# Filter rows ordered by ScalarE before they are turned, late rows turned in pairs, one transform with four residues: a long-convolution and gated-MLP gradient kernel on one core

## The chip, the core and the metric

The kernel runs on one core of a Trainium2 chip. The metric is the device time of one execution in microseconds (us). The five engines are named as in the profile: PE (TensorE; PEld is its weight load), DVE (VectorE), ACT (ScalarE), POOL (GpSimd) and SP (SyncE, which here only issues DMAs). Each engine works through its own instructions in order; semaphores tie the engines together.

## What is computed

The forward pass and all its gradients, for one sequence of S = 2048 rows and D = 1024 columns, F = 3584:

```python
xn = _layernorm(x)                                   # x = A_q
kv = causal_shift(k, shift_k, 4 taps) * v
y  = irfft(rfft(kv, 2S) * rfft(ssm_k, 2S))[:S] + kv * ssm_D      # per column
s  = xn * y
g  = silu(((xn @ w_gate) * (xn @ w_up)) @ w_down)
out = x + s * g
# returned: out and the gradients of x, k, v, shift_k, ssm_k, ssm_D, w_gate, w_up, w_down for grad_out
```

Two parts matter here: the layer norm, with the transposed rows that the product with w_gate and w_up needs, and the Fourier transforms of kv and of the filter ssm_k.

## The kernel before

**Stages.** (1) About 0 to 60 us: the rows of x arrive in six chunks of 1, 1, 2, 4, 4 and 4 blocks of 128 rows. Each chunk is normalised (`layer_norm`) and its rows are transposed into the tiles XNT (U0 to U3), so that they can be the weights of matmuls. (2) Up to about 505 us: slab after slab of w_up and w_gate is multiplied (`gu_unit`, L673: one block is eight matmuls of 128x512 into one of two PSUM buffers `psg`; ACT copies the result out, L675; DVE multiplies its halves into hN; five blocks or more later hN is transposed, L571 or L724). The forward half of the convolution (`conv_forward`) runs between these blocks. (3) About 505 to 700 us: the down projection (L1032) and the gate. (4) From about 700 us: the gradients (L1480, L1497, L1580, L1642).

**The late rows.** The first rows are transposed right behind their normalisation, rows 0 and 1 in two halves (L609), the others whole (L620), and ACT copies them out (L610, L621). All these transposes write one PSUM tile `turns` of four banks, of which `next_bank` hands out one after the other. The chunks of rows 8 to 11 (in U6) and 12 to 15 (in U7) are put on a list and turned by `turn_late`, which `gu_unit` calls behind the first block of a unit: 64 half-transposes for four rows (`turn_halves`, L571: two instructions per 128x128 block, one per 64 partitions) into the whole of `turns`, then four copies by ACT (L631). The layer norm of a chunk is a chain on DVE (statistics L584, L585; L587, L589), one square root on ACT (L592), and DVE again (L595 to L599), which ends in the normalisation of each row (L603).

**The filters.** D is cut into eight slices of 128 columns, ds = 0 to 7. For each one `load_h` brings 128 rows of ssm_k into the first half of U5 as `hrow[p, c, u, r]`: time is 1024c + 8u + r, so that the elements of one residue r lie 8 elements (16 bytes) apart. `h_rows` turns 16 blocks (c, r) with 32 half-transposes. The block is the weight operand of the transpose, so PE itself reads it with that step of 16 bytes. Then ACT copies the result, scaled, into `hx` (L791, two instructions). hx and the shifted product kv of the slice are each transformed: matmuls with a table (`cmm`, L234, 128x256 each), a copy by ACT into SP, then sums on DVE. With eight residues (`fwd8_half`, `fwd8`) this takes 16 matmuls and a longer chain on DVE; with four (`fwd4_half`, `fwd4_sums`, `fwd4_outs`) it takes 32 matmuls and a shorter chain. The list EIGHT names the transforms with eight residues as (slice, 1 for the filter or 0 for kv).

**What sets the order.** A scheduler orders each engine's instructions from the order in which the code issues them and its own costs. The convolution is a generator whose steps yield their planned DVE time; `pump` lets it run ahead in proportion to the blocks that are done (`tick`), with F_TOTAL as the planned whole. DVE's convolution work and some multiplies keep the program's order (`keep_in_program_order`). POOL's queue issues the stores and the loads of k, v and ssm_k.

Of the kernel before, what the change touches and what calls it, by code (L numbers as in the profile page):

```python
# [10 lines left out]
ACT = mybir.ActivationFunctionType  # L11
ALU = mybir.AluOpType
AX = mybir.AxisListType
BF16 = mybir.dt.bfloat16
F32 = mybir.dt.float32
I32 = mybir.dt.int32
PSUM = bass.MemoryType.PSUM


def build_kernel(  # L20
# [498 lines left out]
    fg = pool("fg", 2, side="right")  # L519
    ps_tr = pool("ps_tr", 1, space=PSUM)  # L520
    ps_gu = pool("ps_gu", 2, space=PSUM)
    ps_st = pool("ps_st", 1, space=PSUM)
    turns = ps_st.tile([P, 4, 2, 4, P], BF16, name="tr")
    bank = [0]

    def next_bank():
        bank[0] += 1
        return turns[:, bank[0] % 4]

    busy = turns[:, 0].rearrange("p a b x -> p (a b x)").bitcast(F32).rearrange("p (a x) -> p a x", a=4)  # L530

    def keep_busy(n):
        for i in range(n):
# [33 lines left out]
    def turn_halves(ps, src):  # L567

        for hh in range(2):
            rows = slice(64 * hh, 64 * hh + 64)  # L570
            ins = nc.tensor.transpose(ps(hh), src[rows], ident[rows, rows])  # L571
        return ins

    def halves(x):
        return x.rearrange("p b (h u) -> p h b u", h=2)

    def layer_norm(b0, n, x4):
        def small(name, dt=F32):
            return lns.tile([P, 4], dt, name=name)[:, 0:n]
        mv = lns.tile([P, 4, 2], F32, name="mv")[:, 0:n, :]  # L580
        for i in range(n):
            bst = lns.tile([P, 2, 6], F32, name="bst")
            for hh in range(2):
                V.bn_stats(out=bst[:, hh, :], in_=x4[:, i, hh * 512:(hh + 1) * 512])  # L584
            V.bn_aggr(out=mv[:, i, :], in_=bst[:])  # L585
        var_b = small("var_b", BF16)
        V.tensor_copy(var_b, mv[:, :, 1])  # L587
        vpe = small("vpe", BF16)
        V.tensor_scalar(vpe, var_b, EPS, None, op0=ADD)  # L589
        half_r = small("half_r")  # L590
        with tc.issue_after(act_copy[0].ins) if act_copy[0] is not None else nullcontext():
            root = nc.scalar.activation(half_r, vpe, ACT.Sqrt, scale=0.25)  # L592
        q0 = small("q0")
        rec = small("rec")
        V.reciprocal(rec, half_r)  # L595
        tt(q0, vpe, rec, MUL)
        sq_b = small("sq_b", BF16)
        V.scalar_tensor_tensor(sq_b, q0, 0.25, half_r, op0=MUL, op1=ADD)
        V.reciprocal(RSTD[:, b0:b0 + n], sq_b)  # L599
        for i in range(n):  # L600
            b = b0 + i
            q, qi = divmod(b, 4)
            last = V.tensor_scalar(x4[:, i, :], x4[:, i, :], mv[:, i, 0:1], RSTD[:, b:b + 1], op0=SUB, op1=MUL)  # L603
            if b < 2:
                for hh in range(2):
                    ps = next_bank()[:, 0]
                    for dc in range(4):
                        d0 = (4 * hh + dc) * P
                        tr_ln[0] = nc.tensor.transpose(ps[:, dc, :], x4[:, i, d0:d0 + P], ident[:])  # L609
                    act_copy[0] = nc.scalar.copy(out=XNT[0][:, 4 * hh:4 * hh + 4, b * P:b * P + P], in_=ps)  # L610
                if b == 0:
                    with tc.issue_after(tr_ln[0].ins):
                        keep_busy(10)
                continue
            if b0 >= 8:
                turn_rows.append((x4[:, i, :], q, qi))
                continue
            ps = next_bank().rearrange("p a b x -> p (a b) x")
            for dc in range(DC):
                tr_ln[0] = nc.tensor.transpose(ps[:, dc, :], x4[:, i, dc * P:(dc + 1) * P], ident[:])  # L620
            act_copy[0] = nc.scalar.copy(out=XNT[q][:, :, qi * P:(qi + 1) * P], in_=ps)  # L621
        c, r0 = divmod(b0, 8)
        return last, root, st(xnn[:, c, r0:r0 + n, :], x4[:, 0:n, :])

    def turn_late():
        ps = turns[:].rearrange("p (h j) i b x -> p h j i (b x)", h=2).rearrange("p h j i (a u) -> p h (j i) a u", u=64)
        for i, (x, q, qi) in enumerate(turn_rows):
            for dc in range(DC):
                tr_ln[0] = turn_halves(lambda hh: ps[:, hh, i, dc], x[:, dc * P:(dc + 1) * P])
        for i, (x, q, qi) in enumerate(turn_rows):  # L630
            act_copy[0] = nc.scalar.copy(out=halves(XNT[q][:, :, qi * P:(qi + 1) * P]), in_=ps[:, :, i])  # L631
        turn_rows.clear()

    nop = lambda: None
# [4 lines left out]
    def tr_tile():  # L639
        return ps_tr.tile([P, 2, 8, P], BF16, name="tr")  # L640
# [90 lines left out]
    h_out = []  # L731
    cv_gone = []
    ht_st = [None]
    EIGHT = ((0, 0), (0, 1), (6, 0), (7, 0), (7, 1))
    INV8 = (2, 4, 5, 6, 7)
    SHIFT_W = 8 * 2.3

# [4 lines left out]
    def conv_forward():  # L742
# [33 lines left out]
            st(KSHd[dp], U[6][:].rearrange("p (b d) -> p b d", b=NB))  # L776
            yield 2.3

        def h_rows(ds):
            if ds == 8:  # L780
                return
            hrow = S_["h", ds]
            hx = S_["hx"] = cf.tile([P, NB, P], BF16, name="hx")
            pe_us[0] += 0.67
            ps = tr_tile()[:].rearrange("p h b x -> p h (b x)").rearrange("p h (b u) -> p h b u", u=64)
            with tc.issue_after(tr_ln[0].ins):
                turn_halves(lambda hh: ps[:, hh, 0], hrow[:, 0, :, 0])
            for b in range(1, 16):
                turn_halves(lambda hh: ps[:, hh, b], hrow[:, b // 8, :, b % 8])
            for c in range(2):  # L790
                nc.scalar.activation(halves(hx[:, 8 * c:8 * c + 8, :]), ps[:, :, 8 * c:8 * c + 8], ACT.Copy, scale=WSC)  # L791
            h_out.append(ds)
            if ds + 1 < 8:
                load_h(ds + 1)

        def kvs(ds):
            return S_["kvt", ds // 2][:, :, ds % 2 * P:(ds % 2 + 1) * P]
# [62 lines left out]
        yield from shift(0)  # L860
        PIN[0] = True
        yield 3.9
        h_rows(0)
        yield 0.1
        tl = turn_tables(ps_cv)
        sp = [half(0, S_["hx"], i, Dz[:, 0:P]) for i in range(2)]
        for ds in range(8):
            yield 0.5
            if ds % 2 == 1 and ds < 7:
                with tc.issue_after(S_["kst"].ins):  # L870
                    for c in range(2):
                        load_kv(ds // 2 + 1, c)
            D0 = Dz[:, ds * P:(ds + 1) * P]
            sph = []
            KX = cx.tile([P, 16, 256], BF16, name="KX")
            HX = cs.tile([P, 16, 256], BF16, name="HX", bufs=2)
            own_room = lambda X: X[:].rearrange("p a x -> p (a x)").bitcast(F32).rearrange("p (a x) -> p a x", a=8)[:, 0:4]
            eight = (ds, 1) in EIGHT
            if ds == 0:
                yield from transform(0, 1, sp, HX, own_room(KX), lambda i: sph.append(half(0, kvs(0), i)), nop)  # L880
            else:
                yield from transform(ds, 0, sp, KX, own_room(HX), lambda i: sph.append(half(ds, S_["hx"], i, D0)), nop)
                S_["kst"] = st(KFd[ds], KX[:])
            calls = []

            def behind():
                calls.append(0)
# [3 lines left out]
            yield from transform(ds, int(ds > 0), sph, HX if ds else KX, room, nop1 if eight else lambda c: h_rows(ds + 1) if c == 0 else None,  # L891
                                 behind)
# [80 lines left out]
    st(RSTN[:], RSd.rearrange("(b p) -> p b", p=P))  # L973
    for p_ in (lnp, lns, tg, bsb):
        p_.release()
    ps_st.release()
    ps_cv = pool("ps_cv", 2, space=PSUM)
    pump, drain, step = make_pump(conv, F_TOTAL)
    cnt = [-5]
# [826 lines left out]
```

## Time and profile before

| what | value |
|---|---|
| time, three runs | 1914.03, 1915.66 (median), 1917.43 us |
| the profiled execution | 1915.97 us, of which the span from first to last instruction is 1914.2 us |
| granted PE clock, mean | 0.999 |
| busy: PE, DVE, ACT, POOL | 1895.2, 1550.7, 637.1, 334.8 us |
| PE busy from 100 to 500 us | 397.3 of 400 us |
| PE busy from 20 to 45 us | 19.93 of 25 us |

The profile lists instructions by line of the kernel before, with the tile written and the tiles read (`tr<-ident,U` is a transpose of something in a U tile into the PSUM tile tr). A timeline row gives the start, the time from the first start to the last end of a run of equal instructions, the engine and the line, and in square brackets the idle time of the engine ahead of it with what ended it. A wait row gives the total, the number of times and the longest.

### The profile page before, as it was taken

Reading aid. Unit: us, or ns where it says so; the run is one execution under the profiler, and the core shown is the slowest. Engines: PE = TensorE matmul, PEld = TensorE weight load, DVE = VectorE, ACT = ScalarE, POOL = GpSimd, SP = SyncE. Lnnn points to the kernel's source line nnn. Section 1 sums busy time; section 2 is a strip of 40 time slices with the busy share of each in tenths; the row PEclk is TensorE's granted clock in tenths of the full one; section 3 lists DMA queues with packets and bytes.
Section 4 is the critical chain, followed back from the end, with each engine's and each line's share of the span. In section 5 each row is a group of like instructions: output and inputs, shape, how many; then the busy total and the mean of one; then the engine's idle time right before and its main releaser. Section 6 shows DMA issues by size and latency. Waiting matters only on the chain.

```text
span 1914.2 us, 28265 instructions
## 1 busy us (share of the span) xinstructions
PE 1895.2 (99%) x11367; PEld 1014.8 (53%) x11507; DVE 1550.7 (81%) x1711; ACT 637.1 (33%) x927; POOL 334.8 (17%) x465
## 2 busy tenths in 40 slices
PE   8999999999999999999999999999999999999999
PEld 4555555545444456666666665664444444444444
DVE  7999999999988556887999999999995205678862
ACT  5765555546433233432222222222222102011122
POOL 5121212111113220001031221111212101112120
PEclk9999999999999999999999999999999999999999
DMA  8777866769769997677888698585887999889963
GB/s 285 269 251 232 257 224 207 234 233 296 248 228 311 313 306 230 208 239 229 275 264 264 221 266 267 181 286 177 227 245 173 221 203 180 182 176 195 194 162 124
DMA packets 425107, 444.35 MB, mean 232 GB/s; under 512 B 268400, under 2 KB 342796, under 8 KB 410512
## 3 DMA queue, kind: packets, MB, share of 16 engines
q1 hardware_dynamic: 367504, 239.03, 46.7%
q0 software_dynamic: 41152, 174.15, 29.3%
q10 hardware_dynamic: 16320, 29.36, 4.1%
q8 instruction: 90, 1.47, 0.3%
q14 instruction: 41, 0.34, 0.1%
HBM read 193.87 MB, written 189.84 MB: 200 GB/s over the span
## 4 chain that ended last, share of the span: by engine, by line
PE 96%; DVE 1%; issue 1%; ACT 1%; DMA 1%; SPq 0%; ACTq 0%; DVEq 0%
PE psb L1497 20%; PE psx L1642 20%; PE psg L673 19%; PE psb L1480 10%; PE psb L1580 9%; PE psbm L1032 9%; PE psF L234 3%; PE tr L571 1%; PE psI L455 1%; PE psY L1191 1%; PE psY L445 1%; PE psx L1580 1%; DMA U<-in_A_q_dram 1%; ACT U L631 0%; DVE bst L584 0%
## 5 line engine op out<-in xcount | busy, mean ns | idle before, releaser
L673 PE MATMUL psg<-wslab,U 128*128 128x512 bf16 x1728 | 399.0, 380 | 5.2 <-ACT gut L675 1.2
L1497 PE MATMUL psb<-U,U 128*128 128x512 bf16 x1792 | 397.1, 379 | 0.0
L1642 PE MATMUL psx<-U,dgut 128*128 128x512 bf16 x1505 | 331.0, 379 | 1.6
L1642 PEld LDWEIGHTS <-dgut 128*128 128x128 bf16 x1792 | 175.3, 98 | 211.4
L1497 PEld LDWEIGHTS <-U 128*128 128x128 bf16 x1792 | 175.2, 98 | 198.0
L673 PEld LDWEIGHTS <-U 128*128 128x128 bf16 x1792 | 172.4, 98 | 195.0 <-issue 3.5
L1480 PE MATMUL psb<-wdt,U 128*128 128x256 bf16 x1792 | 205.6, 273 | 0.0
L1480 PEld LDWEIGHTS <-U 128*128 128x128 bf16 x1792 | 175.3, 98 | 29.2
L212 DVE TENSOR_TENSOR W<-W 128x1024 f32<-128x1024 f32 (+1 forms) x189 | 186.5, 1003 | 4.1
L1580 PE MATMUL psb<-U,U 128*128 128x512 bf16 x797 | 176.1, 379 | 0.9
L1502 ACT CAST wb<-psb 128x512 bf16<-128x512 f32 x112 | 65.6, 586 | 315.4 <-PE psb L1497 313.4
L1247 DVE SCALAR_TENSOR_TENSOR dkp<-dkT,kT 128x1024 bf16<-128x1024 bf16 (+2 forms) x64 | 78.3, 1224 | 97.7 <-DMA dkT<-DKSHd 96.0
L1032 PE MATMUL psbm<-U,ht 128*128 128x512 bf16 x658 | 145.0, 379 | 0.7
L1580 PEld LDWEIGHTS <-U 128*128 128x128 bf16 x896 | 87.4, 98 | 104.3
L675 ACT CAST gut<-psg 128x512 bf16<-128x512 f32 x156 | 91.6, 589 | 117.0 <-PE psg L673 108.9
L1674 ACT ACTIVATE dx_t<-dxn 128x1024 bf16<-128x1024 f32 x15 | 15.9, 1057 | 323.1 <-DVE dxn L212 317.7
L1032 PEld LDWEIGHTS <-ht 128*128 128x128 bf16 x672 | 65.6, 98 | 78.2
L212 DVE TENSOR_TENSOR U<-U,dht 128x2048 bf16<-128x2048 bf16 x56 | 68.3, 1221 | 46.8 <-ACT dht L1482 46.7
L1482 ACT CAST dht<-psb 128x512 bf16<-128x512 f32 x112 | 65.6, 587 | 116.3 <-PE psb L1480 116.3
L66 POOL DMA_DIRECT2D Hd<-hN x54 | 37.3, 690 | 261.2 <-DVE hN L212 259.0
L1621 ACT CAST wbs<-psb 128x512 bf16<-128x512 f32 x51 | 29.9, 586 | 145.4 <-PE psb L1580 134.4
L212 DVE TENSOR_TENSOR W<-SP 128x1024 f32<-128x1024 f32 x64 | 74.2, 1218 | 1.6 <-ACT SP L295 1.1
(259 smaller groups left out, 2342.2 us busy)
## 6 DMA issues: line engine op xcount, KB each, us to landing
U<-GUd SPq DMA_DIRECT2D x28, 1024.0 KB, 8.9
DGd<-U SPq DMA_DIRECT2D x28, 1024.0 KB, 6.2
GUd<-gut ACTq DMA_DIRECT2D x39, 512.0 KB, 5.8
out_dram<-wb SPq DMA_DIRECT2D x112, 128.0 KB, 4.9
U<-Hd SPq DMA_DIRECT2D x14, 1024.0 KB, 6.7
Hd<-hN POOLq DMA_DIRECT2D x54, 256.0 KB, 5.0
HTd<-hT SPq DMA_DIRECT2D x24, 512.0 KB, 4.1
ht<-HTd SPq DMA_DIRECT2D x18, 512.0 KB, 7.6
```

What stands on the lines that cost most here:

```text
L212: pinned(V.tensor_tensor(o, a, b, op))
L234: mm = nc.tensor.matmul(ps[:, k].rearrange("p (c d) -> p c d", c=2), T[:, r, k, :], xr[:, r], start=(n == 0), stop=(n == len(rs) - 1 and ( ...
L673: gu_mm[0] = nc.tensor.matmul(ps[:], XNT[q][:, dc, qi * P:(qi + 1) * P], w[:, dc].rearrange("p a f -> p (a f)"), start=(dc == 0), stop=(dc ...
L675: nc.scalar.copy(out=gut[:, :, i], in_=ps[:].rearrange("p (a f) -> p a f", a=2))
L1032: mm = nc.tensor.matmul(ps[:, dh * 512:(dh + 1) * 512], ht(fc)[:, i * P:(i + 1) * P], WD[fc // 4][:, fc % 4, dh * 512:(dh + 1) * 512], sta ...
L1247: ins = V.scalar_tensor_tensor(prod[:].rearrange("p r d -> p (r d)")[:, lo:H], dkT[:, 0, lo:H], 1.0, kT[:, 0, 13 + m + lo:13 + m + H], op0 ...
L1480: nc.tensor.matmul(ps[:, x * SLW:(x + 1) * SLW], DBMT[2 * hf + g][:, dc, (b % 4) * P:(b % 4 + 1) * P], wdt[:, dc, :], start=(dc == 0), sto ...
L1482: nc.scalar.copy(out=dht[:, 2 * e:2 * e + 2].rearrange("p b f -> p (b f)"), in_=ps[:])
L1497: nc.tensor.matmul(ps[:], XN[b // 4][:, b % 4, dc * P:(dc + 1) * P], dgus[b // 8][:, :, b % 8], start=(b == 0), stop=(b == NB - 1))
L1502: nc.scalar.copy(out=wb[:, dc % 2].rearrange("p a f -> p (a f)"), in_=ps[:])
L1580: nc.tensor.matmul(ps, h[:, f, b, :], DBM[b // 4][:, b % 4, dh * 512:(dh + 1) * 512], start=(b == 0), stop=(b == NB - 1))
L1642: nc.tensor.matmul(ps[:, dh * 512:(dh + 1) * 512], t[n][:, f, i * P:(i + 1) * P], WGU[n][:, f, dh * 512:(dh + 1) * 512], start=(n == 0 and ...
```

## The change

- The first transposes get PSUM buffers of their own: the tile `turns` becomes a pool of four single-bank buffers.
- `turn_late` releases that pool and takes one with two buffers of two banks, each for two rows: two rows are turned and copied, then the next two.
- For slices 1 to 7 the filter rows are first ordered by residue: ACT reads hrow with the step of 16 bytes and writes hx (`h_order`, scaled, two instructions). Then the 32 half-transposes read hx, whose elements are contiguous, and ACT copies the result back into hx (`h_turn`). The two halves of the work are called at two steps of the convolution. Slice 0 keeps the order of before, but with 16 whole transposes in place of 32 half ones.
- (6, 0) leaves EIGHT: kv of slice 6 is transformed with four residues.

```diff
-    ps_st = pool("ps_st", 1, space=PSUM)
-    turns = ps_st.tile([P, 4, 2, 4, P], BF16, name="tr")
+    ps_st = [pool("ps_st", 4, space=PSUM)]
...
-                    ps = next_bank()[:, 0]
+                    ps = ps_st[0].tile([P, 4, P], BF16, name="tr")
...
-            ps = next_bank().rearrange("p a b x -> p (a b) x")
+            ps = ps_st[0].tile([P, DC, P], BF16, name="tr")
...
     def turn_late():
-        ps = turns[:].rearrange(...)
-        for i, (x, q, qi) in enumerate(turn_rows):
-            for dc in range(DC):
-                tr_ln[0] = turn_halves(lambda hh: ps[:, hh, i, dc], x[:, dc * P:(dc + 1) * P])
-        for i, (x, q, qi) in enumerate(turn_rows):
-            act_copy[0] = nc.scalar.copy(out=halves(XNT[q][:, :, qi * P:(qi + 1) * P]), in_=ps[:, :, i])
+        if turn_rows and len(ps_st) == 1:
+            ps_st[0].release()
+            ps_st.append(pool("ps_s2", 2, space=PSUM))
+        for i in range(0, len(turn_rows), 2):
+            ps = ps_st[1].tile([P, 2, 2, DC, 64], BF16, name="tr2")
+            for j, (x, q, qi) in enumerate(turn_rows[i:i + 2]):
+                for dc in range(DC):
+                    tr_ln[0] = turn_halves(lambda hh: ps[:, hh, j, dc], x[:, dc * P:(dc + 1) * P])
+            for j, (x, q, qi) in enumerate(turn_rows[i:i + 2]):
+                act_copy[0] = nc.scalar.copy(out=halves(XNT[q][:, :, qi * P:(qi + 1) * P]), in_=ps[:, :, j])
...
-    EIGHT = ((0, 0), (0, 1), (6, 0), (7, 0), (7, 1))
+    EIGHT = ((0, 0), (0, 1), (7, 0), (7, 1))
...
-        def h_rows(ds):
+        def h_order(ds):
...
+            if ds > 0:
+                for c in range(2):
+                    nc.scalar.activation(hx[:, 8 * c:8 * c + 8, :], hrow[:, c].rearrange("p u r -> p r u"), ACT.Copy, scale=WSC)
+                if ds + 1 < 8:
+                    load_h(ds + 1)
+
+        def h_turn(ds):
...
+            if ds == 0:
+                ps = tr_tile()
+                for b in range(NB):
+                    ...
+                        nc.tensor.transpose(ps[:, b // 8, b % 8, :], hrow[:, b // 8, :, b % 8], ident[:])
+                    if b % 8 == 7:
+                        nc.scalar.activation(hx[:, b - 7:b + 1, :], ps[:, b // 8], ACT.Copy, scale=WSC)
+                load_h(1)
+            else:
+                ps = tr_tile()[:]...
+                for b in range(NB):
+                    turn_halves(lambda hh: ps[:, hh, b], hx[:, b, :])
+                for c in range(2):
+                    nc.scalar.copy(out=halves(hx[:, 8 * c:8 * c + 8, :]), in_=ps[:, :, 8 * c:8 * c + 8])
...
-            yield from transform(..., nop1 if eight else lambda c: h_rows(ds + 1) if c == 0 else None, behind)
+            yield from transform(..., nop1 if eight else lambda c: (h_order, h_turn)[c](ds + 1), behind)
...
-            if eight:
-                h_rows(ds + 1)
+            if eight:
+                h_order(ds + 1)
...
-            yield from product(KX, HX, KX, cs, False, 0)
+            steps = product(KX, HX, KX, cs, False, 0)
+            yield next(steps)
+            if eight:
+                h_turn(ds + 1)
+            yield from steps
```

More of the change, by code (lines that the diff above doesn't have):

```diff
@@ L521, in build_kernel @@
     ps_gu = pool("ps_gu", 2, space=PSUM)
-    ps_st = pool("ps_st", 1, space=PSUM)
-    turns = ps_st.tile([P, 4, 2, 4, P], BF16, name="tr")
[L524 to L530, printed above, removed]
+    ps_st = [pool("ps_st", 4, space=PSUM)]
+    busy = ps_st[0].tile([P, 4, P], F32, name="tr")
     def keep_busy(n):
@@ L609, in layer_norm @@
                         tr_ln[0] = nc.tensor.transpose(ps[:, dc, :], x4[:, i, d0:d0 + P], ident[:])
-                    act_copy[0] = nc.scalar.copy(out=XNT[0][:, 4 * hh:4 * hh + 4, b * P:b * P + P], in_=ps)
+                    act_copy[0] = nc.scalar.copy(out=XNT[0][:, 4 * hh:4 * hh + 4, b * P:b * P + P], in_=ps[:])
                 if b == 0:
@@ L617, in layer_norm @@
                 continue
-            ps = next_bank().rearrange("p a b x -> p (a b) x")
+            ps = ps_st[0].tile([P, DC, P], BF16, name="tr")
             for dc in range(DC):
                 tr_ln[0] = nc.tensor.transpose(ps[:, dc, :], x4[:, i, dc * P:(dc + 1) * P], ident[:])
-            act_copy[0] = nc.scalar.copy(out=XNT[q][:, :, qi * P:(qi + 1) * P], in_=ps)
+            act_copy[0] = nc.scalar.copy(out=XNT[q][:, :, qi * P:(qi + 1) * P], in_=ps[:])
         c, r0 = divmod(b0, 8)
@@ L625, in turn_late @@
     def turn_late():
-        ps = turns[:].rearrange("p (h j) i b x -> p h j i (b x)", h=2).rearrange("p h j i (a u) -> p h (j i) a u", u=64)
-        for i, (x, q, qi) in enumerate(turn_rows):
-            for dc in range(DC):
-                tr_ln[0] = turn_halves(lambda hh: ps[:, hh, i, dc], x[:, dc * P:(dc + 1) * P])
-        for i, (x, q, qi) in enumerate(turn_rows):
-            act_copy[0] = nc.scalar.copy(out=halves(XNT[q][:, :, qi * P:(qi + 1) * P]), in_=ps[:, :, i])
+        if turn_rows and len(ps_st) == 1:
[8 more added lines that the diff above has]
+                act_copy[0] = nc.scalar.copy(out=halves(XNT[q][:, :, qi * P:(qi + 1) * P]), in_=ps[:, :, j])
         turn_rows.clear()
@@ L783, in h_rows @@
             hx = S_["hx"] = cf.tile([P, NB, P], BF16, name="hx")
-            pe_us[0] += 0.67
[L785 to L791, printed above, removed]
+            if ds > 0:
[4 more added lines that the diff above has]
+        def h_turn(ds):
+            if ds == 8:
+                return
+            hx = S_["hx"]
+            pe_us[0] += 0.67
+            if ds == 0:
+                hrow = S_["h", 0]
+                ps = tr_tile()
+                for b in range(NB):
+                    with tc.issue_after(tr_ln[0].ins) if b == 0 else nullcontext():
+                        nc.tensor.transpose(ps[:, b // 8, b % 8, :], hrow[:, b // 8, :, b % 8], ident[:])
[3 more added lines that the diff above has]
+            else:
+                ps = tr_tile()[:].rearrange("p h b x -> p h (b x)").rearrange("p h (b u) -> p h b u", u=64)
+                for b in range(NB):
+                    turn_halves(lambda hh: ps[:, hh, b], hx[:, b, :])
+                for c in range(2):
+                    nc.scalar.copy(out=halves(hx[:, 8 * c:8 * c + 8, :]), in_=ps[:, :, 8 * c:8 * c + 8])
             h_out.append(ds)
-            if ds + 1 < 8:
-                load_h(ds + 1)
         def kvs(ds):
@@ L862, in conv_forward @@
         yield 3.9
-        h_rows(0)
+        h_order(0)
+        h_turn(0)
         yield 0.1
@@ L890, in conv_forward @@
             room = cf.tile([P, 4, 256], F32, name="room", tag="hx")[:] if eight else None
-            yield from transform(ds, int(ds > 0), sph, HX if ds else KX, room, nop1 if eight else lambda c: h_rows(ds + 1) if c == 0 else None,
+            yield from transform(ds, int(ds > 0), sph, HX if ds else KX, room, nop1 if eight else lambda c: (h_order, h_turn)[c](ds + 1),
                                  behind)
@@ L975, in build_kernel @@
         p_.release()
-    ps_st.release()
+    ps_st[1].release()
     ps_cv = pool("ps_cv", 2, space=PSUM)
```

## The prediction

> **What bounds the kernel.** I read the busy times first, then the chain that ended last, then PE's waits.
>
> ```profile
> PE 1895.2 (99%) x11367; PEld 1014.8 (53%) x11507; DVE 1550.7 (81%) x1711; ACT 637.1 (33%) x927; POOL 334.8 (17%) x465
> ...
> PE 96%; DVE 1%; issue 1%; ACT 1%; DMA 1%; SPq 0%; ACTq 0%; DVEq 0%
> ...
> PE tr L620 <- DVE U L603: 3.2, 1, 3.2
> PE psg L673 <- ACT gut L675: 1.2, 1, 1.2
> PE tr L609 <- ACT U L610: 0.9, 2, 0.7
> ```
>
> PE is the bound from the first microseconds to the end. So the change can win in two ways only: less time of PE's own instructions, or less of PE's idle time, which lies almost all ahead of 60 us. Other engines matter where they make PE wait. The timeline of PE gives the prices:
>
> ```profile
> 147.56 1.17 PE L571 MATMUL tr<-ident,U 64*128 64x64 bf16 x32
> 148.66 1.90 PE L673 MATMUL psg<-wslab,U 128*128 128x512 bf16 x7
> ...
> 155.69 0.64 PE L571 MATMUL tr<-ident,hN 64*128 64x64 bf16 x32
> 156.27 1.04 PE L673 MATMUL psg<-wslab,U 128*128 128x512 bf16 x3
> ...
> 471.14 1.04 PE L234 MATMUL psF<-kv,TF 128*128 128x256 bf16 x8
> 472.01 5.34 PE L673 MATMUL psg<-wslab,U 128*128 128x512 bf16 x24
> ```
>
> From the start of a group to the start of the next: 32 half-transposes of filter rows (tile U, step of 16 bytes) hold PE for 1.10 us, 32 of hN (contiguous) for 0.58, unrounded 1.098 and 0.574. Eight transform matmuls cost 0.87. The weight loads say why; in one stretch of 100 us:
>
> ```profile
> L571 PEld LDWEIGHTS <-hN x160: 92/95/96, 311.7 to 388.4; 64*128 64x128 bf16 x160
> L571 PEld LDWEIGHTS <-U x64: 137/165/170, 322.9 to 374.7; 64*128 64x128 bf16 x64
> ```
>
> The start is shown by rows of DVE, PE and ACT:
>
> ```profile
> 18.63 1.88 DVE L584 BATCH_NORM_STATS2 bst<-U 128x6 f32<-128x512 bf16 x3 [2.00 <-DMA U<-in_A_q_dram]
> 20.43 1.04 DVE L212 TENSOR_TENSOR hN_s<-gut_s 128x256 bf16<-128x256 bf16 x1
> 21.39 0.20 DVE L585 BATCH_NORM_AGGREGATE mv<-bst 128x2 f32<-128x12 f32 x1
> ...
> 27.00 0.62 PE L620 MATMUL tr<-ident,U 128*128 128x128 bf16 x8 [3.19 <-DVE U L603]
> ...
> 36.03 0.22 ACT L592 ACTIVATE half_r<-vpe 128x4 f32<-128x4 bf16 x1
> 39.53 3.76 ACT L631 COPY U<-tr 128x1024 bf16<-128x1024 bf16 x4 [1.77 <-PE tr L571]
> ...
> 43.83 3.61 PE L673 MATMUL psg<-wslab,U 128*128 128x512 bf16 x16 [1.21 <-ACT gut L675]
> ```
>
> A multiply of 0.28 us (its neighbours at 16.15 and 16.35) takes 1.03 at 20.43, in the middle of the layer norm of rows 4 to 7 and beside POOL's four copies of 17.06 to 21.27. PE waits 3.19 us for that chain. The next chunk's square root stands ready at 34.98 and runs at 36.03, behind two copies of ACT. Then four copies of ACT in a row keep PE waiting for 1.21 us.
>
> **1. Filter rows.** Seven slices go from 1.098 to 0.574 us on PE: 7 x 0.524 = **-3.7**. Slice 0 gets 16 whole strided transposes for 32 half ones: between a contiguous whole one (0.056, L620) and a load that nothing overlaps (0.163, the median strided load), 0.9 to 2.6 us against 1.1. I take the pair of strided halves, 1.098/16 = 0.069 each: **0**, bounds -0.2 and +1.5.
>
> Added on ACT: 14 activations that read with the step of 16 bytes. No row has ACT reading so. From below: a contiguous activation of 1024 elements, 1.04 us (L964); from above: twice that. ACT is 57% busy from 100 to 500 us, so the 15 to 29 us fit. Behind each one waits the copy of a slab block (0.59), and PE waits for that copy when it is late by more than ACT's usual idle time of 1.14 us ahead of it, since PE fills the other PSUM buffer in 1.73. The built order of the changed kernel spreads them: the two of a slice have a slab copy between them, and in most slices 16 transform matmuls (0.87 to 1.75 us) follow on PE before the buffer is wanted. Laid out by hand for slices 2 to 4 with 1.04, and for 2 and 4 with 2.08, PE keeps a margin of 0.1 us or more. So **0**; without that cover, 14 x (2.08 - 1.14) = +13. Below 0 it can't go, nothing is taken from ACT's path. The transposes of hx wait for ACT, but stand a step of the convolution (several blocks of 1.73) behind. On POOL each `load_h` now waits for ACT instead of PE; its data are wanted a slice, some 50 us, later, and the waits of that kind (POOL U L66 <- PE tr L571) total 13.3 us today without holding PE.
>
> **2. Slice 6.** 16 more matmuls of 128x256, two groups of 0.87: **+1.75** on PE. DVE loses about 6 us: the chain with eight residues at 74.62 to 90.96, less a multiply of 0.61, takes 15.7; the one with four has the same first 4.6 and four sums of 1.22. DVE isn't on the path; it gets slack, of which part 3 takes some. PE's tightest DVE input is a kv tile, ready 1.47 us ahead of its matmuls at 302.93; by counting both orders PE comes to them 1.35 later in its own work and DVE has one multiply (0.6) more, so the wait stays away. 0, or up to +1 if DVE lags.
>
> **3. The start**, laid out on the new order with old durations. First half-rows: PE no longer waits for ACT (0.67 and 0.24), but the first matmuls of the second slab still wait for its DMA at 14.59: nothing gained yet. Rows 4 to 7: the slow multiply now stands ahead of the statistics, in DVE's idle 2.00 us, so the chain ends 0.96 earlier, and rows are ready at 26.0, 26.45, 26.9 and 27.35. PE has 41 matmuls of 0.216 and 18 transposes of 0.055 from 14.59 on, arrives at 24.4, and finishes the four rows at 27.9. Then 29 matmuls and six small transposes: 34.5. DVE's next chain is 0.96 earlier, and 0.20 for a wait at 34.02 that falls away: its square root stands ready at 33.8. ACT has done its copies at 32.3, so it runs at once, 2.2 earlier than 36.03. Row 8 is ready at 35.5, row 11 at 36.8; PE waits 1.0 and has turned them at 37.2. ACT copies the first two rows from 36.3 to 38.15, the others to 40.0, the slab block to 40.5: PE goes on at 40.5 where it was 43.83. **-3.3**. The same pairing at rows 12 to 15 takes the wait of 0.34 at 57.89: **-0.3**. Bounds: 0, if the slab, the rows' DMA or another multiply sets the pace again; and -7, all idle time from 23.8 to 58 us (5.3) and half of the 3.4 us at half clock. I stay with the schedule, which lies between. Everything later keeps step: DVE starts its shift some 3.4 earlier, since what it waits for (ACT's copy, PE's turn, k's load behind a store of rows 8 to 11) moves too.
>
> A row on the clock: the granted clock of 28.0 to 31.4 us, right behind PE's wait of 3.19, is 0.51. [...] If it halves again, PE loses up to 1.7 of work, of which the wait of 1.0 at 34.5 hides 1.0: +0.7.
>
> **Sum.** -3.7 + 0 + 1.75 - 3.3 - 0.3 = -5.5 us. The profiled execution took 1915.97 (span 1914.2, 1.77 around it), 0.3 over the median of 1915.66. Forecast: **1910.4**.
>
> **Rivals.**
> A, the start gives nothing back: another wait replaces the one at 27.00. For: DMA is nearly full there, and the rows of a chunk are now turned together, so PE waits for the last of four. Against: the rows land at 18.6 and the chain is DVE's own. -3.7 + 1.75: 1914.0.
> B, the turn isn't faster, because writing into PSUM and not the weight load sets 1.10 us: -3.6 + 1.75: 1914.1. Against: the two L571 groups differ in the weights' step alone.
> C, slower: ACT's strided read costs as PE's does. Longest strided to contiguous load, 173/95: 1.89 us each. If the slab copy stands right behind each, PE waits 0.75 at each of 14: +10.5, so 1920.9. It eats the whole gain from 1.53 us per activation on (5.5/14 over 1.14) and is slower by over 0.2% from 1.79, if the cover counted in part 1 fails at nearly all of them.
> [...]
>
> **Chances.** Forecast 0.63, A 0.2, B 0.05, C 0.12. Range 1907.9 to 1915: below, a start that gains 5.9 and slice 0 at -0.2 (1907.9); above, A with slice 0 at +1.5 (1915.5, cut a little); C is left out. About 0.2% (3.8 us, to 1911.8) is what a measurement can tell from no change. Forecast falls under faster, A and B under same, C under slower.
>
> **What would show it.** Half-transposes of hx at 0.57 us a group; PE's wait near 27 us halved and the waits of 0.67 and 1.21 gone or shorter, the block of 43.83 near 40.5; 32 matmuls for kv of slice 6; the ordering activations near 1.04 us; no new PE wait on ACT. A wait `PE psg <- ACT` counted some 14 times would make it wrong (C), as would a wait on L603 that stays at 3 us (A).

## The result: 1921.5 us, slower than before by 0.3%

The changed kernel took **1921.52 us** (median of 8 runs, 1919.65 to 1923.69) beside 1915.28 for the kernel before in the same job (8 runs): ratio 1.0031, interval 1.0021 to 1.0040. Forecast were 1910.4, and a range up to 1915. The profiled execution took 1923.45, span 1921.7 against 1914.2 before.

The first part of the page and PE's waits (total, times, longest) of the changed kernel, in its profiled execution:

```profile
PE 1901.1 (99%) x11507; PEld 1011.7 (53%) x11507; DVE 1544.9 (80%) x1699; ACT 662.2 (34%) x941; POOL 334.6 (17%) x465
```

```profile
PE psg L671 <- ACT U L673: 6.3, 4, 2.3
PE psx L1661 <- DVE dxn L212: 2.6, 1, 2.6
PE psg L671 <- ACT gut L673: 2.2, 4, 0.9
...
PE tr L614 <- DVE U L597: 0.9, 1, 0.9
```

PE's busy time can't be set against the 1895.2 of before: that profile lists 11367 of PE's instructions beside 11507 weight loads, this one 11507 of each. Before, PE's only wait above 1.5 us was the one of 3.2 in the start. That one is now 0.9 (1.6 forecast). In its place stand waits of the slab product (`psg`) for ACT. The ordering activations and the copy behind the turn, from the rows of the tile hx:

```profile
L784 ACT ACTIVATE hx<-U x14: 2045/2130/2150, 103.6 to 448.9; 128x1024 bf16<-128x1024 bf16 x14
L807 ACT COPY hx<-tr x14: 1012/1017/1042, 112.8 to 455.0; 128x1024 bf16<-128x1024 bf16 x14
```

2.13 us (median) with the step of 16 bytes, 1.02 for as many elements without it. The forecast had taken 1.04 and looked at 2.08 for two slices only. Slice 1 is the worst place; first ACT's timeline, then PE's:

```profile
103.56 2.08 ACT L784 ACTIVATE hx<-U 128x1024 bf16<-128x1024 bf16 x1 [2.66 <-DVE KX L283]
105.54 0.58 ACT L673 CAST U<-psg 128x512 bf16<-128x512 f32 x1
106.00 1.88 ACT L193 COPY TI<-psT 128x2048 bf16<-128x2048 bf16 x1
107.76 2.04 ACT L784 ACTIVATE hx<-U 128x1024 bf16<-128x1024 bf16 x1
```

```profile
102.73 1.89 PE L671 MATMUL psg<-wslab,U 128*128 128x512 bf16 x8
106.17 1.89 PE L671 MATMUL psg<-wslab,U 128*128 128x512 bf16 x8 [1.55 <-ACT U L673]
110.33 1.89 PE L671 MATMUL psg<-wslab,U 128*128 128x512 bf16 x8 [2.28 <-ACT U L673]
```

ACT stands still for 2.66 us in front of the first activation, because hx of slice 1 gets the buffer that DVE still uses as scratch (`room`, tag "hx", L905) for the eight-residue transform of slice 0. The slab copies (L673, from psg) queued behind are late, PE has filled both PSUM buffers and waits 1.55 and 2.28 us.

To see where the time goes, I compared the start of the same slab block in both traces (the 16th, the 32nd and so on; each block has 8 weight loads): after minus before is -3.9 us at the 16th and -4.0 at the 32nd (the start has won), -0.3 at the 48th (slice 1 has taken 3.7 back), and +3.3 at the first matmul of the down projection. From there it stays +3.3 to 1610 us, where a wait of 2.57 and a stretch at a granted clock of 0.57 make it +7.5. (That is the profiled execution, one of the slowest of the eight; the medians lie 6.2 apart.)

### The profile page after: what moved, and what is told of

Its sections match the earlier page's. It is cut to its first block, busy times and chain, and to the rows that moved or that the text cites. A ratio compares the mean times of both kernels' runs of the same rounds, so it can differ in the third digit from the quotient of the medians.

```text
span 1921.7 us, 28410 instructions
## 1 busy us (share of the span) xinstructions
PE 1901.1 (99%) x11507; PEld 1011.7 (53%) x11507; DVE 1544.9 (80%) x1699; ACT 662.2 (34%) x941; POOL 334.6 (17%) x465
## 5 line engine op out<-in xcount | busy, mean ns | idle before, releaser
L673 ACT CAST gut<-psg 128x512 bf16<-128x512 f32 x156 | 91.6, 592 | 117.7 <-PE psg L671 108.4
```

What stands on the lines that cost most here:

```text
L673: nc.scalar.copy(out=gut[:, :, i], in_=ps[:].rearrange("p (a f) -> p a f", a=2))
```

## Experiments

Ratios stand against the kernel before, run in the same job. Waits, leads and lines are of one profiled execution of each kernel. The lead is how much earlier than before the same slab block starts.

**Rows as before: start and four residues only**

```diff
 # the change without h_order / h_turn
-            h_order(ds + 1) ... h_turn(ds + 1)
+            h_rows(ds + 1)
```

> The changed kernel with the filter rows turned as before (PE reads them with the step of 16 bytes, ACT orders nothing); the new start and the four residues of slice 6 stay. Theory READ: the 14 ordering activations of the changed kernel take 2.13 us each, twice what a contiguous read takes, and PE then waits for slab copies queued behind them, 8.1 us in all between 100 and 480 us. Then this kernel gets the start's -3.9 and the +1.75 of slice 6: 1915.3 - 3.9 + 1.75 = 1913.1, and PE has no wait on ACT over 0.5 us after 60 us. Rival PACE: the smaller planned total and the four residues move the convolution's steps against the slab blocks, and that makes PE wait, whatever ACT reads: about 1921, with the waits of the changed kernel.

Measured 1915.23, ratio 1.0002 (0.9993 to 1.0011). Without the ordering 6 us of loss are gone; the new pace alone doesn't make the loss. But it is 2 above READ, and PE waits 0.68 us for ACT at 472 us, where READ had nothing over 0.5.

**Rows only**

```diff
 # the kernel before, with h_order / h_turn and nothing else of the change
-            h_rows(ds + 1)
+            h_order(ds + 1) ... h_turn(ds + 1)
```

> The kernel before with the ordering and turning of the filter rows alone changed. READ: -3.7 on PE for the turn, +8.1 or a little more of waits on ACT: 1919.7 to 1921, with ordering activations of 2.1 us and PE waiting behind them by 1 to 2 us in several slices. PACE: no such waits, 1915.3 - 3.7 = 1911.6.

Measured 1920.95, ratio 1.0032 (1.0019 to 1.0044). The ordered rows by themselves cost as much as the whole change, with eight residues in slice 6 too. READ's time holds. Its 8.1 us of waits are 6.6 here: 1.36 and 1.51 in slice 1, the second for hx itself at the turn, and the rest near 265, 380 and 451 us.

**Start only**

```diff
 # the kernel before, with the PSUM pool and turn_late of the change only
-    turns = ps_st.tile([P, 4, 2, 4, P], BF16, name="tr")
+    ps_st = [pool("ps_st", 4, space=PSUM)]
```

> The kernel before with the transposes of the first and late rows alone changed (own PSUM buffers, turned in pairs). READ and PACE alike: the start's -3.9 stays to the end, 1911.4, since PE is the bound throughout. Rival GIVEN BACK: PE that is ahead meets the same later time of a DMA (as it waits for DVE near 1612 us in the changed kernel), and the end moves by less than 1 us: 1914.5 to 1915.3.

Measured 1912.00, ratio 0.9986 (0.9978 to 0.9995). The lead is 3.1 us at the 32nd block and 3.1 at the end: nothing is given back.

**Ordering activation with a contiguous read**

```diff
-hx[:, 8 * c:8 * c + 8, :], hrow[:, c].rearrange("p u r -> p r u")
+hx[:, 8 * c:8 * c + 8, :].rearrange("p b u -> p (b u)"), hrow[:, c].rearrange("p u r -> p (u r)")
```

> The changed kernel, but the 14 ordering activations read the filter rows contiguously, so the rows are not ordered by residue and the filter's values are mixed up; every instruction and tile is otherwise the same. READ: the activations take 1.04 us, PE's waits behind them go, but for slice 1, where ACT stands 2.7 us waiting for DVE: 1915.3 - 3.9 - 3.7 + 1.75 = 1909.5, up to 1911.8 with that wait. PACE: the step of the read does not matter, about 1921.

Measured 1916.66, ratio 1.0009 (1.0000 to 1.0018). The activation takes 1.07 us (median) in place of 2.13, and the kernel is 4.9 us faster than the changed one, where READ had some 10 to 12: READ is half right. PE's waits that are left:

```profile
PE psg L671 <- ACT gut L673: 3.9, 4, 1.7
PE psg L671 <- ACT U L673: 1.9, 2, 1.3
```

Of the first row 0.94 and 0.20 lie ahead of 75 us; the others stand in slice 1 (0.57, 1.31) and slice 7 (1.69, 1.03). So a pair of activations makes PE wait even at half the length, where ACT is busy or held up anyway. From here on the theory is LOAD: not the length alone, but where the added work stands in ACT's queue.

**Four residues only**

```diff
-    EIGHT = ((0, 0), (0, 1), (6, 0), (7, 0), (7, 1))
+    EIGHT = ((0, 0), (0, 1), (7, 0), (7, 1))
```

> The kernel before with (6,0) taken from the list EIGHT and nothing else. LOAD (the loss of the whole change is PE waiting for slab copies of ACT that stand behind the added ordering activations; the four residues cost their 16 matmuls alone): 1915.2 + 1.8 = 1917.0. Rival FOUR (the kernel with the start and the four residues was timed 3.2 us over the one with the start alone, so the four residues also bring a wait in slice 7): 1918.4 or more, with a PE wait on ACT near 470 us.

Measured 1918.38, ratio 1.0017 (1.0008 to 1.0026): 3.5 over before, FOUR's side of the two. PE's own work grows by 1.8, as forecast; a wait of 1.03 near 474 us on ACT is new. In ACT's timeline:

```profile
469.58 1.07 ACT L675 CAST gut<-psg 128x512 bf16<-128x512 f32 x2 [3.77 <-DMA GUd<-gut]
```

ACT's slab copy can't write, because a store of the buffer `gut` has not landed; then two slab copies, two into hT and two into the tile SP (not the engine) stand in a row, 4.6 us, until the next slab copy at 474.16. Before, the same wait of ACT was 2.47 us and cost PE nothing.

**Own scratch for slice 0**

```diff
-room = cf.tile([P, 4, 256], F32, name="room", tag="hx")[:] if eight else None
+room = (U[7][:, 0:2048].bitcast(F32)... if ds == 0 else cf.tile([P, 4, 256], F32, name="room", tag="hx")[:]) if eight else None
```

> The changed kernel, with DVE's scratch tile 'room' of slice 0 in U7 instead of the buffer that hx of slice 1 needs, so that the first ordering activation of slice 1 no longer waits 2.66 us for DVE. LOAD: the two PE waits of slice 1 (1.55 and 2.28) shrink by about 2.6 together, all other waits on ACT stay: 1921.5 - 2.6 = 1918.9. Rival STRIDE ALONE (the two waits come from the 2.05 us of each activation, the wait for DVE lay beside other work): 1921.5, the two waits as before. Where the late dkT transpose of the changed kernel's profile (PE wait of 2.57 and a half clock behind it, 4.1 together) is chance, it is absent in some profiles, and the time is up to 4 lower in either case.

Measured 1915.93, ratio 1.0005 (0.9997 to 1.0014), 5.6 below the changed kernel. The activations still take 2.12 us, but both waits of slice 1 are gone (3.8 us, more than LOAD's 2.6), and so, in this profile, is the late wait at 1610 us. The two waits don't make up all of the 5.6; the rest may be that late wait, which the median of the changed kernel can hold in part, but no run shows it apart. What is left on ACT, but for one of 0.20 at 74 us, stands in slices 4 (0.76, 0.74), 6 (1.70) and 7 (0.22, 0.84).

**Ordering on POOL**

```diff
-nc.scalar.activation(hx[...], hrow[:, c].rearrange("p u r -> p r u"), ACT.Copy, scale=WSC)
+nc.gpsimd.tensor_copy(hx[...], hrow[:, c].rearrange("p u r -> p r u"))
```

> The start of the change and its filter rows, kv of slice 6 with eight residues as before, but POOL orders the filter rows (the scale moves to ACT's copy behind the turn). LOAD: ACT has no added work, so PE keeps the whole gain of the turn: 1912.0 (start alone) - 7 x 0.524 = 1908.3, with no PE wait on ACT above 1 us after 60 us. Rival PORT (POOL's copies, about 2 us each by half the 4.1 us of its 128x2048 copies, slow DVE beside them as they slowed a multiply from 0.28 to 1.03 us, and PE waits for DVE): 1910 or more, with PE waits on DVE in slices 1 to 7. Rival KEPT (the turn of contiguous rows gives PE nothing on the whole): 1912.

Measured 1952.93, ratio 1.0197 (1.0183 to 1.0211). Wrong by 45 us for LOAD, and not as PORT had it either: POOL is the one that is held up. Rows of the copy, then of PE's waits:

```profile
L784 POOL COPY hx<-U x14: 1974/2400/20214, 104.2 to 480.9; 128x1024 bf16<-128x1024 bf16 x14
```

```profile
PE tr L565 <- POOL hx L784: 27.6, 6, 13.2
```

One copy took 20.2 us, from 388.7 us on, and PE waited 13.2 us for it; DVE was busy for 18.4 of them. The next copy, with DVE idle, took 1.97. But the twelve others, beside a busy DVE too, took 2.1 to 10.0 us, and what makes the difference was not tried.

**Four pieces behind slab copies**

```diff
+            slab = nc.scalar.copy(out=gut[:, :, i], in_=...)
+            if pieces:
+                with tc.issue_after(slab.ins):
+                    pieces.pop(0)()          # 128x512, half of one activation
...
+            h_order(ds + 1)                  # ahead of the second transform; room of slice 0 in U7
```

> The start and the filter rows with eight residues for slice 6; ACT orders as in the change, but in four pieces of 512 elements a slice (about 1.07 us each by half of 2.13), each placed right behind one slab copy, the first a step of the convolution earlier ('room' of slice 0 in U7). ACT has the same work as in the change. LOAD: a piece fits into ACT's usual idle time of 1.14 us behind a slab copy, so the waits of the pairs go: 1908.3 to 1910. Rival TOTAL (ACT's added 29 us, not where it stands, makes PE wait): 1914 or more, with PE waits on ACT of some 5 us in all after 100 us.

Measured 1917.35, ratio 1.0017 (1.0008 to 1.0026). A miss for LOAD as forecast, but the waits have changed:

```profile
PE tr L565 <- ACT hx L788: 3.9, 6, 1.1
...
PE tr L565 <- ACT hT L709: 1.8, 2, 0.9
```

From 60 to 500 us the slab blocks wait for ACT only twice, by 0.20 and 0.32. PE now waits at the turn, for the last piece.

**Every slice another step**

```diff
+R = (8, 8, 2, 4, 16, 32, 8, 1)
-hrow[:, c].rearrange("p u r -> p r u")
+hrow[:, c].rearrange("p u r -> p (u r)").rearrange("p (u r) -> p r u", r=R[ds])
```

> The changed kernel with another step of reading in each slice's two ordering activations (slices 1 to 7: 16, 4, 8, 32, 64, 16 and 2 bytes), 1024 elements and the same place in the program each time; the filter values are mixed up by it. [...] Rival STEP (the cost grows with the step): between 1.07 and 2.13 at 4 and 8 bytes, above 2.13 at 32 and 64. [...]

Measured 1920.19, a single execution. ACT's timeline gives the second activation of slices 1, 3 and 4, with steps of 16, 8 and 32 bytes:

```profile
108.01 2.04 ACT L786 ACTIVATE hx<-U 128x1024 bf16<-128x1024 bf16 x1
...
209.92 1.20 ACT L786 ACTIVATE hx<-U 128x1024 bf16<-128x1024 bf16 x1
...
262.42 2.13 ACT L786 ACTIVATE hx<-U 128x1024 bf16<-128x1024 bf16 x1
```

Slices 2 (4 bytes) and 7 (2 bytes) took 1.06 and 1.07, slice 5 (64 bytes) 2.00 and 2.05, slice 6 (16 bytes) 2.11 and 2.07. PE's waits of slices 1, 4 and 6 stayed as they were in the changed kernel. STEP falls: the cost doesn't grow with the step. 4 bytes cost no more than 2, 8 bytes 1.20, and 16, 32 and 64 bytes all about double (2.00 to 2.13).

**Pieces, and the turn a step later**

```diff
 # over the kernel with four pieces
-lambda c: h_turn(ds + 1) if c else None        # in the transform
+nop1
...
             yield next(steps)                   # first step of the product
-            if eight:
-                h_turn(ds + 1)
+            h_turn(ds + 1)
```

> The kernel with four pieces a slice, and the turn of the ordered rows one step of the convolution later in every slice (behind the first step of the product), so that PE comes to it when the last piece is done. LOAD: the waits of the hx turn for ACT (3.9 in all) go, the slab copies stay on time: 1917.4 - 3.9 - some of the 1.8 of waits for hT's copy = 1912 to 1913.5. If the turn of contiguous rows gives PE its whole 3.7 and no wait takes its place: 1908.3. Rival MOVED (what PE doesn't wait for at the turn it waits for at the next copy of ACT, since the same 33 us of ACT lie in the same stretch): 1916 or more.

Measured **1910.31**, ratio 0.9979 (0.9970 to 0.9988): faster than before and than the changed kernel. From 60 to 500 us PE has no wait above 0.2. The pieces took 1.16 us each, so ACT does even more work than in the change. MOVED falls: the same amount of ACT's work in the same slices costs PE no wait up to 500 us when each piece stands behind a slab copy, slice 0 has its own scratch and PE comes late enough.

**Own scratch and contiguous read**

```diff
 # over the kernel with own scratch: the contiguous read from above
-hrow[:, c].rearrange("p u r -> p r u")
+hrow[:, c].rearrange("p u r -> p (u r)")
```

> The changed kernel with 'room' of slice 0 in U7 and, besides, the ordering activations reading their rows contiguously (the order is left out, the filter values are mixed up). LOAD: without the doubled length the waits of slices 4 and 6 (0.76, 0.74 and 1.70) go as well, those of slice 7 stay (1.1 to 2.7, one of about 0.7 to 1.0 is of the four residues): 1915.9 - 3.2 = 1912.7, up to 1914 if slice 7 waits as with the contiguous read before. Rival STRIDE NOTHING (with the wait for DVE gone, the length of the activation no longer matters): 1915.9.

Measured 1914.27, ratio 0.9995 (0.9986 to 1.0004). The waits of slices 4 and 6 (3.2 us) are gone, as LOAD has it; slice 7 takes 2.91 and 1.03, near LOAD's upper case. ACT's timeline there:

```profile
460.10 0.52 ACTq L72 DMA_DIRECT2D GUd<-gut  x1
466.73 1.07 ACT L673 CAST gut<-psg 128x512 bf16<-128x512 f32 x2 [6.66 <-DMA GUd<-gut]
```

The store that ACT waits for was issued at 453.19 and landed 12.9 us after its issue had ended (in the kernel before, the store issued at 448.60 took 7.5). It went out right behind SP's loads of HTd into U at 451.45; that these delay it was not tried. In the four kernels with the ordering in pairs and four residues at the same pace, the waits of slice 7 grow with the lead at the 192nd block: 1.0 us in all at a lead of 1.3, 1.1 at 5.2, 2.7 at 6.7 and 3.9 here at 9.3. The kernel with pieces and the late turn (eight residues, lead 6.1) has none, so the lead alone doesn't make them.

**The whole change with the good place**

```diff
 # the kernel with pieces and the late turn, and
-    EIGHT = ((0, 0), (0, 1), (6, 0), (7, 0), (7, 1))
+    EIGHT = ((0, 0), (0, 1), (7, 0), (7, 1))
```

> The whole change (start, ordered filter rows, four residues for kv of slice 6), with the one difference from it that ACT's ordering stands where the last kernel has it: four pieces behind slab copies, the turn a step later, 'room' of slice 0 in U7. PLACE (the change lost its gain by where ACT's ordering stands, not by the strided reads as such, nor by the four residues beyond their matmuls): 1910.3 + 1.8 = 1912.1, up to 1913.1 with the wait of 0.7 to 1.0 in slice 7 that two kernels with four residues showed. Rival FOUR (the four residues bring DVE's chains and ACT's copies of slice 7 together so that more is lost): 1914 or more, with PE waits on ACT of 2 us or more near 465 to 475 us.

Measured 1916.66, ratio 1.0009 (1.0000 to 1.0018): 4.9 below the changed kernel, but 4.6 above PLACE. PE waits 0.91 and 0.91 for copies of hT, 2.00 at 351 us and 1.65 at 468 us. The one at 351, in ACT's timeline:

```profile
348.72 1.93 ACT L709 COPY hT<-tr 128x1024 bf16<-128x1024 bf16 x2 [2.96 <-DMA HTd<-hT]
```

Again ACT stands behind a store that has not landed (hT has one buffer), and the slab copies behind it are late.

**The same, at the pace of eight residues**

```diff
-    F_TOTAL += len(EIGHT) * (FWD8_W - 9.6 + 0.95 * 1.75) - 2.0
+    F_TOTAL += (len(EIGHT) + 1) * (FWD8_W - 9.6 + 0.95 * 1.75) - 2.0
```

> The kernel with four residues and well placed pieces, with the planned whole of the convolution (F_TOTAL) as with eight residues for slice 6, so that its steps stand against the blocks of the slab product as in the kernel of pieces and late turn (1910.3). PACING (the four residues cost 4.5 us beyond their matmuls because a smaller F_TOTAL moves every step of all slices to other blocks, and there ACT's copies meet stores that haven't landed): 1910.3 + 1.8 = 1912.1 to 1913.2, the PE waits at 153, 331 and 351 us gone, one in slice 7 possible. Rival WORK (the second 16 matmuls and SP copies themselves bring the waits): 1915 or more.

Measured 1916.98, ratio 1.0012 (1.0003 to 1.0021). Half of PACING is right: the waits at 153, 331 and 351 us are gone, and at the 176th block the lead is 6.3 us (6.1 in the best kernel). Then, in slices 6 and 7 (from the 176th to the 208th block), all of it and more goes:

```profile
PE psg L672 <- DMA wslab<-in_B_w_gate_dram: 3.5, 2, 2.5
PE psF L234 <- ACT SP L256: 1.6, 1, 1.6
```

The wait of 2.5 for the slab's own load (at 455 us) is followed by a stretch of 3.4 us at a granted clock of 0.56, which costs some 1.5 more (an estimate: 3.4 x 0.44). Together with the 16 matmuls (1.8) that is about 7.4 of the 7.9 us that are lost there. By time alone WORK wins; by the trace, pace and work each have their part.

**The changed kernel at the pace of before**

```diff
 # the changed kernel with the F_TOTAL of the diff above
```

> The changed kernel with the same planned whole as before (F_TOTAL counted with five transforms of eight residues). PACING: the waits of slices 4, 6 and 7 come at other places or sizes; those of slice 1 (3.8) stay, since hx waits for 'room' there; the four residues no longer shift all steps: 1921.5 less up to 4. Rival PLACE ALONE (the ordering pairs make PE wait wherever they stand): 1920 to 1922, waits on ACT of 7 us or more in all.

Measured 1922.78, ratio 1.0037 (1.0024 to 1.0051). Pace doesn't save the changed kernel. The waits for ACT above 0.3 us, after 60 us, sum to 5.8 (1.38, 1.50, 0.75, 0.74, 1.38), under PLACE ALONE's 7; one of 2.95 for a slab's load comes on top.

**Nothing but the pace**

```diff
 # the kernel before with the F_TOTAL of the diff above
```

> The kernel before with nothing changed but the planned whole: F_TOTAL counted with one transform of eight residues more than there are, so that the convolution's steps stand against other blocks by as much as the change moves them, the other way. Its work is the same. PACING alone, without ordering on ACT: if the places matter by themselves, PE waits on ACT or DVE of 1 us or more come up and the time is 1916.5 or more. Rival MARGIN (without the ordering on ACT there is room enough at any pace, the waits need both): 1914.9 to 1915.7.

Measured 1925.11, ratio 1.0052 (1.0039 to 1.0065). MARGIN falls: a convolution that is planned faster, with the same work, costs 10 us by itself. Two waits of 0.66 and 1.01 come up by 362 us, and then PE's largest, in its timeline:

```profile
512.15 0.41 PE L571 MATMUL tr<-ident,hN 64*128 64x64 bf16 x16
517.42 0.61 PE L571 MATMUL tr<-ident,hN 64*128 64x64 bf16 x16 [4.86 <-DVE hN L212]
```

PE waits for DVE's product hN of a late slab. DVE works in the order of the program, so what is planned earlier stands ahead of such products; that this is the reason was only argued. So F_TOTAL has an effect at its far end that is larger than the whole change; which value is best was not tried.

## Why the prediction was wrong, step by step

**The step that failed** is the one in part 1 that puts the 14 added activations at "So **0**": "the two of a slice have a slab copy between them, and in most slices 16 transform matmuls [...] follow on PE", "Laid out by hand for slices 2 to 4 with 1.04, and for 2 and 4 with 2.08, PE keeps a margin". After 60 us PE waits 8.3 us for ACT in the changed kernel, in eight places. What the step had wrong:

- The slab copy between the two activations of a slice isn't always there. In slice 6 a copy of yf stands in its place (ACT's rows below), and PE waits 1.70 us. The layout by hand had stopped at slice 4.
- Slice 4 was laid out, at 2.08, with a margin of 0.1 or more, and PE waits 0.77 and 0.74 us there. Behind the second activation stand two copies of hT and one of yf before the next slab copy. The turn of hx, which the prediction had put several blocks behind ACT, waits the 0.77 for those copies of hT. Where the layout had them isn't on record.
- Slice 1 was left out. There hx shares a buffer with DVE's scratch, and a tile that is allocated a step earlier waits for whoever still has the buffer. Own scratch takes 3.8 us of waits away.
- The length. Rival C had the right cause, ACT's strided read, and nearly the right price (1.89, measured 2.13), but made it depend on all 14 activations failing alike. Contiguous reads take 3.2 us of waits away in slices 4 and 6. The upper bound of the prediction, twice 1.04, was nearly the truth. That C's 1920.9 lies so near the 1921.52 is luck: its 14 waits of 0.75 aren't there, and the slice 1 wait for DVE, slice 7 and the late loss (below) are not in it.
- ACT's idle time isn't free to be used up: late stores (`gut`, `hT`) take it too, in slice 7 and, in another kernel, at 351 us. The cover of 1.14 us is the usual value, and there are places without it.

ACT's timeline in slice 6, from the first ordering activation to the next slab copy:

```profile
376.30 2.11 ACT L784 ACTIVATE hx<-U 128x1024 bf16<-128x1024 bf16 x1
378.28 1.03 ACT L823 CAST yf<-psI 128x1024 bf16<-128x1024 f32 x1
379.17 2.11 ACT L784 ACTIVATE hx<-U 128x1024 bf16<-128x1024 bf16 x1
381.14 1.10 ACT L673 CAST U<-psg 128x512 bf16<-128x512 f32 x2
```

**The rest of part 1** is right: the turn takes 0.57 us from start to start (150.87 to 151.45 us) in place of 1.10, and slice 0 takes 0.98. The gain is real: in the kernel at 1910.31 the lead grows from 3.4 us at the 32nd block to 6.6 at the first matmul of the down projection, 3.2 of the 3.7. There 0.9 is lost again (PE waits 0.72 at 505 us for DVE's product hN), so the span is 1908.5 against 1911.1 with the start alone.

**Part 2**: +1.8 on PE, as forecast; "0, or up to +1 if DVE lags" came out as 0.7 to 1.0, from ACT behind a late store and not from DVE. No run shows a use of DVE's slack.

**Part 3**: -4.0 in the changed kernel for a forecast of -3.6, and the wait of 3.19 became 0.89. PE goes on at 39.89 us (40.5 forecast). Rival A falls; the gain is kept to the end in the kernel with the start alone. B falls with the turn's 0.57. Two things in the -4.0 are not the schedule. The rows had landed at least 0.7 us earlier (DVE's statistics begin at 17.92, 18.63 before); in the kernel with the start alone they begin at 19.13, PE's wait is 1.90 and the gain 3.1. And the profile of before has the 3.4 us at a granted clock of 0.51 behind its wait. The kernel with four residues alone has the start of before and no such stretch: PE waits 2.65 there, runs on at the full clock (an estimate: its mean granted clock of 0.999 leaves room for one slow stretch, and that one, at 0.60, starts at 1612.9 us), and is 2.1 us ahead of before at the 16th block. So some 1.5 us of the gain (2.1 less 0.5 of shorter wait) is that stretch falling away, which the sum counted on when it took the full clock; against an execution of before without the stretch the start gains less. That the clock stays whole behind a wait of 1.6 us was shown by no run when the sum was made; in the changed kernel the granted clock was 1.00 behind the wait of 0.89 (25.3 to 28.7 us) and behind the one of 1.70 in slice 6 (381.8 to 385.2).

**Not foreseen at all** was the late loss, in the profiled execution of the changed kernel. A transposed load on SP's queue comes late, DVE waits for it, and PE waits for DVE (timeline of PE, then its windows with busy time and granted clock ahead of the DMA columns):

```profile
1614.52 3.72 PE L1661 MATMUL psx<-U,dgut 128*128 128x512 bf16 x10 [2.57 <-DVE dxn L212]
```

```profile
1611.90:1614.50 2.60, 0.05 (x1) 0.90 1.16 253
1614.50:1617.90 3.40, 3.38 (x10) 0.57 1.12 275
```

Behind 2.57 us of waiting stand 3.4 us at 0.57 of the clock: 4.1 us in all. The profile of the four residues alone shows it too (3.17); in all others it is absent, or 0.3 at most. The eight transposed loads from 1515.8 us on hold SP's queue for 19.7 us (16.0 before), beside six transfers of POOL that start in that time; that these delay them was only argued. The kernel with the contiguous read has 20.1 us for the same eight loads and loses only 0.3. What goes with the loss is how late the second load of dkT lands: 83.6 and 84.2 us behind the first matmul of this stage in the two profiles that lose, 76.1 to 81.2 in the other fifteen. The other executions of the changed kernel took from 1919.7, about what 1923.45 less 4.1 gives, to 1923.7, so this loss seems to come in some executions and not in others. The loss up to 505 us (+3.3) doesn't depend on it.

**The sum.** Forecast -5.5, measured +7.5 in span: 13.0 apart. Waits for ACT after 60 us are 8.3 of it, the late loss 4.1, the start -0.4. That leaves 1.0, which lies in how a wait is counted. In PE's rows of slice 1 above, eight matmuls start at 102.73. At the 0.216 us from one to the next that the prediction uses, the ninth could start 1.73 us later; it starts at 106.17, 3.44 later. So 1.71 us are lost where the wait row says 1.55: the row of matmuls lasts 1.89, 0.16 beyond the moment at which PE could go on. At eight waits that is 1.3 us, and the sum closes within 0.3. What decides whether four residues for slice 6 can be had for their 1.8 us stays open: at both paces that were tried they cost about 6.5 beside the best kernel.

## What to carry to other kernels

Where one engine is busy 99% of the time, work that is moved to an engine with half its time free is hidden only where it stands between two things that the bound engine waits for; lay out every place where it is put, the first and the last slice above all, with the buffers that it takes and the stores that free them. Cut it into pieces about as long as the usual gap (here 1.16 us beside 1.14), pin each behind an instruction that just freed the bound engine, and let the consumer come a step later: here that, with a scratch buffer of its own for slice 0, turned a loss of 5.7 us (rows only) into a gain of 1.7 over the start alone. A planned pace in the code is part of the tuning, and any change of the work that it plans needs a look at its far end.

## What the runs showed of the hardware that was not expected

- ACT read 1024 bf16 elements per partition in 1.06 to 1.07 us at steps of 2 and 4 bytes, 1.19 to 1.20 at 8, and 2.00 to 2.15 at 16, 32 and 64 (the changed kernel and the one with other steps).
- A POOL copy of 128x1024 with a step of 16 bytes took 1.97 us with DVE idle and 2.1 to 20.2 us beside a busy DVE (median of all 14: 2.4).
- Waits of PE of 2.51, 2.57, 2.62 and 2.95 us were followed by some 3.4 us at a granted clock of 0.55 to 0.57, others of 2.28 and 2.91 us by 1.00, and one of 2.65 by no such stretch. So between 2.51 and 2.95 us the length of the wait alone didn't decide it here.
- The stores of one tile (`gut`, 39 in the kernel with own scratch and contiguous read) landed 3.0 to 13.9 us after the start of their issue, and ACT, which has to write that buffer again, stood still for up to 6.66 us.
